# Block-sparse attention followed by a gated MLP on one core: probability transposes moved from TensorE to DMA, with converting loads, three score banks and a reordered start

## The chip, the cores and the metric

One core of a Trainium2 chip runs the whole program. The metric is the device time of one execution in microseconds (us). Below, PE is TensorE's matmuls and PEld its weight loads, DVE is VectorE, ACT is ScalarE, POOL is GpSimd, SP is SyncE; "SPq" or "POOLq" is the queue of instructions that such an engine issues, DMA issues above all.

## What is computed

Attention with a block mask (blocks of 32 rows, 24 blocks): a block sees itself and its neighbours, the first and the last block, and three sampled blocks; the first and the last block see everything. An MLP with a swish gate follows.

```python
batch, n_heads, seq, head_dim = (4, 8, 768, 64)
n_tokens, d_model, d_ff = (3072, 512, 2048)

scores = scale * np.matmul(q, k.transpose(0, 1, 3, 2))
mask = np.abs(blk_i - blk_j) <= window                     # window = 1
mask = mask | (blk_i == 0) | (blk_j == 0) | (blk_i == n_blocks - 1) | (blk_j == n_blocks - 1)
for qb in range(n_blocks):
    for kb in sampled_blocks[qb]:                          # three per block
        mask[qb * block:(qb + 1) * block, kb * block:(kb + 1) * block] = True
scores = np.where(mask, scores, -1000000000.0)
attn = softmax(scores)
x = (attn @ v) as (tokens, heads * head_dim)
h = x @ w_in
g = h * (1.0 / (1.0 + np.exp(-beta * h)))
out = g @ w_out
```

All inputs and the output are float32; the kernel works in float16 with float32 accumulation.

## The kernel before

**Tiles.** A batch's 768 queries are six chunks `c` of 128 (four blocks, index `j`). The eight heads go in two quads `Q` of four. A step is (batch, chunk, quad): 48 steps, twelve per batch, in the order of the list `steps`. The chunks come as 1, 2, 0, 5, 3, 4 (`CHUNK_ORDER`); chunks 0 and 5 hold the first and the last block, which need full rows.

**One step.** `scores` (matmuls on line 329) writes two score tiles `sc`, each one PSUM bank: for every block 96 window columns straight from `kT`, and 160 columns from `KG`, a gathered copy of K with the first block, three sampled blocks and the last block. DVE takes the negated maxima `nm` (line 334), ACT the exponentials `probs` (line 337), 128 x 1024 in float16. `probs_T` turns them with eight PE transposes (line 345) into the PSUM tile `tp_p`, which DVE copies to `probsT` (line 349). `attend` multiplies `probsT` by gathered V rows, `VA` (window and first block) and `VB` (sampled and last block), into `av` (line 397); V carries a column of ones, so the sums of the softmax come with it, and lines 415 and 416 divide. The full rows have their own path, `global_scores` (line 361, exponentials on line 375) and `global_T` (six transposes, line 384, and a DVE copy, line 387), four units per batch. `x_transpose` (lines 439 and 441) prepares the MLP's input when both quads of a chunk are done.

**MLP.** Chunks are grouped (`sizes`). For a group, `h_unit` does four matmuls (line 453), a tanh on ACT (line 457) and the gate on DVE (line 459); `o_unit` does half of a chunk's second product, eight matmuls (line 470), and with the second half ACT copies the result out (line 476). The units wait in `moe_q`, and `run_moe` spreads them over the steps, so that PE has matmuls while it waits for attention.

**Order.** The order on PE, POOL and SP is the order of the program text (`tc.manual_schedule`); DVE and ACT are placed by a scheduler. An engine takes its instructions in order, so that a waiting one holds up what stands behind it. `pend_T` and `pend_A` keep the transposition and the attend of a step behind its scores: a step's probabilities are transposed one step later, and attended about two steps later.

**Loads.** `load_quad` brings float32 K, Q or V into staging tiles. `prep_tensor` casts K and Q (ACT and DVE at the start, POOL later, line 212); `transpose_pair` makes `kT` and `qT` with six transposes of two heads at once (line 219) and an ACT copy (line 223). `prep_v` casts V, and `write_vtab` writes it to a table in HBM, `vtab` (line 239). `gather_v` reads rows of it: SP issues `VA` (lines 283, 286, 289) and `VB` (lines 294, 297, and one transfer per block and sample on line 300, their addresses held in registers), or, for chunk 1 alone, POOL issues four indirect transfers (line 280). `gather_chunk` builds `KG` on POOL (lines 255 and 261). The weights come as float32 into big staging tiles, w_in in two halves (line 179) and w_out in two (line 186), and DVE casts them (lines 181 and 188; w_out is halved there, which belongs to the tanh form of the gate).

**PSUM banks.** Scores two, transposes two (`tp_p`, `tp_g`, `tp_k`, `tp_q`, `tp_x` share them), `av` one, MLP three.

Of the kernel before, what the change touches and what calls it, by code (L numbers as in the profile page):

```python
# [20 lines left out]
def kernel(  # L21
# [30 lines left out]
    stage_pool = ctx.enter_context(tc.tile_pool(name="stage", bufs=3))  # L52
    half_pool = ctx.enter_context(tc.tile_pool(name="half", bufs=2))
# [14 lines left out]
    sc_psum = ctx.enter_context(tc.tile_pool(name="sc_psum", bufs=2, space=bass.MemoryType.PSUM))  # L68
    tp_psum = ctx.enter_context(tc.tile_pool(name="tp_psum", bufs=2, space=bass.MemoryType.PSUM))
# [86 lines left out]
    nc.vector.tensor_copy(out=idx_b, in_=idx_f)  # L156
# [18 lines left out]
    HF = D_FF // 2  # L175

    def load_w_in(hf, eng):
        wst = big("w_in_st").rearrange("p (c f) -> p c f", c=N_DMC)
        eng.dma_start(out=wst, in_=w_in_r[:, :, hf * HF:(hf + 1) * HF])
        for f0 in range(0, HF, 256):  # L180
            nc.vector.tensor_copy(out=w_in_sb[:, :, hf * HF + f0:hf * HF + f0 + 256],
                                  in_=wst[:, :, f0:f0 + 256])

    def load_w_out(hf):
        wst = big("w_out_st").rearrange("p (c m) -> p c m", m=D_MODEL)
        nc.gpsimd.dma_start(out=wst, in_=w_out_r[:, 8 * hf:8 * hf + 8, :])
        for c0 in range(0, 8, 2):
            nc.vector.tensor_scalar(out=w_out_sb[:, 8 * hf + c0:8 * hf + c0 + 2, :],
                                    in0=wst[:, c0:c0 + 2, :], scalar1=0.5, scalar2=None,
                                    op0=ALU.mult)  # L190
# [10 lines left out]
    def prep_tensor(name, b, Q, startup):  # L201
        st = st_tiles.pop((name, b, Q))
        h16 = half_pool.tile([P, 6, 4, D], FP16, tag="h16", name=f"{name}16")
        for h in range(4):
            dst = h16[:, :, h, :]
            src = st[:, h, :, :]
            if startup and name == "k":
                nc.scalar.copy(out=dst, in_=src)
            elif startup:
                nc.vector.tensor_copy(out=dst, in_=src)  # L210
            else:
                nc.gpsimd.tensor_copy(out=dst, in_=src)  # L212
        return h16

    def transpose_pair(name, b, Q, pr, h16):
        dstT = (qT if name == "q" else kT)[b]
        tp = tp_psum.tile([P, 1024], FP16, tag="tp", name=f"tp_{name}")
        for e in range(6):
            nc.tensor.transpose(out=tp[:, e * P:(e + 1) * P],  # L219
                                in_=h16[:, e, 2 * pr:2 * pr + 2, :].rearrange(  # L220
                                    "p h d -> p (h d)"),
                                identity=identity)
# [5 lines left out]
    def prep_v(b, Q, startup):  # L228
        st = st_tiles.pop(("v", b, Q))
        for h in range(4):  # L230
            eng = nc.vector if startup else nc.gpsimd
            last = eng.tensor_copy(out=v16[b][:, :, 4 * Q + h, 0:D], in_=st[:, h, :, :])
        return last
# [15 lines left out]
    def gather_chunk(b, c, KG, p0, p1):  # L249
# [3 lines left out]
        k_regs = load_regs(sb_raw, ET.Pool, NB - 1, c)  # L253
        for col, src in ((0, 0), (128, S - BLK)):
            nc.gpsimd.tensor_copy(  # L255
                out=KG[:, j0:j1, p0:p1, col:col + BLK],
                in_=kv[:, p0:p1, src:src + BLK].unsqueeze(1).to_broadcast(
                    [P, j1 - j0, p1 - p0, BLK]))
        for j in js:
            for r in range(3):  # L260
                last = nc.gpsimd.tensor_copy(  # L261
                    out=KG[:, j, p0:p1, BLK * (1 + r):BLK * (2 + r)],
                    in_=kv[:, p0:p1, bass.ds(k_regs[(4 * c + j, r)] * BLK, BLK)])
        return last

    def gather_v(b, c, indirect=False):
# [11 lines left out]
        if indirect:  # L278
            for j in js:
# [10 lines left out]
        if indirect:  # L290
            return VA, VB
        v_regs = load_regs(sb_eff, ET.SP, NB, c)
        gb = [j for j in js if 4 * c + j != NB - 2]
        nc.sync.dma_start(out=VB[96:128, gb[0]:gb[0] + len(gb), :],
                          in_=rows(S - BLK, BLK, 0, len(gb)))
        if len(gb) != nj:
            nc.sync.dma_start(out=VB[96:128, NB - 2 - 4 * c, :], in_=tab[S:S + BLK, :])
        for j in js:
            for r in range(3):
                nc.sync.dma_start(  # L300
                    out=VB[BLK * r:BLK * (r + 1), j, :],
                    in_=tab[bass.ds(v_regs[(4 * c + j, r)] * BLK, BLK), :])
# [38 lines left out]
    def probs_T(pt):  # L341
        tp = tp_psum.tile([P, 1024], FP16, tag="tp", name="tp_p")
        for u in range(4):
            for half in range(2):
                nc.tensor.transpose(out=tp[:, u * 256 + half * P:u * 256 + (half + 1) * P],  # L345
                                    in_=pt[:, u, half * P:(half + 1) * P],
                                    identity=identity)
        ptT = p_pool.tile([P, 4, 2, P], FP16, tag="probsT", name="probsT")
        nc.vector.tensor_copy(out=ptT.rearrange("p u h q -> p (u h q)"), in_=tp)  # L349
# [31 lines left out]
    def global_T(pg):  # L381
        tp = tp_psum.tile([P, 1024], FP16, tag="tp", name="tp_g")
        for ct in range(6):
            nc.tensor.transpose(out=tp[:, ct * P:(ct + 1) * P],
# [332 lines left out]
```

## Time and profile before

| | |
|---|---|
| median of 3 runs | 397.03 us (396.07 to 399.94) |
| profiled execution, own time | 399.42 us |
| its span | 397.6 us |
| mean granted PE clock | 0.966 |
| busy: PE, PEld, DVE, ACT, POOL | 310.0, 181.8, 239.3, 202.0, 170.6 us |
| moved by DMA | 61.24 MB, mean 154 GB/s |
| probs transposes on PE (line 345) | 384, 33.9 us |
| their copies on DVE (line 349) | 48, 32.2 us |
| global transposes on PE (line 384), copies on DVE (line 387) | 9.7 us, 8.8 us |
| K and Q transposes on PE (line 219), both | 192, 19.6 us |
| K and Q casts on POOL (line 212), both | 48, 23.4 us |
| weight casts on DVE (lines 181, 188) | 9.1 us, 5.7 us |
| indirect V gathers issued by POOL (line 280) | 16, 15.6 us |

The busy times come from the profile of one execution; matmuls overlap each other, so a busy PE is not PE at its peak. Where a stage is looked at alone, the busy time of each engine in that stretch of the span is asked for, and the waits and the chain are those that the profile infers from semaphores.

### The profile page before, as it was taken

To read this page: it belongs to the slowest core of one execution; us is meant where nothing else is said; L and a number is where in the kernel's file an instruction comes from. 1 tells how busy PE (TensorE), PEld (TensorE's weight loads), DVE (VectorE), ACT (ScalarE), POOL (GpSimd) and SP (SyncE) were. 2 spreads that over 40 slices of the span, in tenths; PEclk is the share of its full clock that TensorE was granted. 3 is DMA by queue.
4 is the path that set the end of the run, shared out by engine and by line. 5 is a ranking of instruction groups with operands and counts; after the bars stand their busy time and mean duration, and the time that the engine had idled before them with its cause. 6 is when DMAs were issued, how large, how long until landed. Compare 5 with 4: busy or idle time off the path is not lost.

```text
span 397.6 us, 12930 instructions
## 1 busy us (share of the span) xinstructions
PE 310.0 (78%) x5056; PEld 181.8 (46%) x5056; DVE 239.3 (60%) x499; ACT 202.0 (51%) x401; POOL 170.6 (43%) x472
## 2 busy tenths in 40 slices
PE   1433525685757778978988789999799999999996
PEld 0221313574544435444544455555454555445652
DVE  0938746864777664564777565667677767544330
ACT  3461313375645655542656666546555656444441
POOL 4748939957785194037780193082420400000000
PEclk9999999999978988996999999999899999999999
DMA  7798999756897233057983152454313424100112
GB/s 214 284 335 175 368 357 388 242 110 162 269 333 200 53 88 77 8 144 225 330 292 83 44 136 44 116 156 116 104 26 91 128 57 123 41 28 30 51 54 79
DMA packets 41085, 61.24 MB, mean 154 GB/s; under 512 B 7968, under 2 KB 31648, under 8 KB 41024
## 3 DMA queue, kind: packets, MB, share of 16 engines
q1 hardware_dynamic: 29136, 29.01, 27.9%
q0 software_dynamic: 6368, 25.11, 18.1%
q10 hardware_dynamic: 5520, 6.30, 4.6%
q8 instruction: 40, 0.66, 0.8%
q14 instruction: 21, 0.17, 0.1%
HBM read 50.77 MB, written 9.62 MB: 152 GB/s over the span
## 4 chain that ended last, share of the span: by engine, by line
PE 50%; DVE 23%; ACT 10%; DMA 8%; issue 3%; POOL 3%; another core or an unknown queue 1%; POOLq 0%; SPq 0%; ACTq 0%; DVEq 0%
PE ops L470 17%; PE hps L453 17%; DVE nm L334 6%; DMA w_out_st<-in_moe_w_out_dram 4%; DVE g L459 4%; PE sc L329 3%; PE tp_p L345 3%; ACT gp L375 3%; ACT t_sb L457 3%; ACT probs L337 3%; PE av L397 3%; DVE probsT L349 2%; DMA st_q<-in_q_dram 2%; PE av L409 2%; DVE gnm L369 2%
## 5 line engine op out<-in xcount | busy, mean ns | idle before, releaser
L337 ACT ACTIVATE probs<-sc,nm 128x256 f16<-128x256 f32 x192 | 75.5, 475 | 84.1 <-DVE nm L334 83.1
L459 DVE SCALAR_TENSOR_TENSOR g<-t_sb,hps 128x512 f16<-128x512 f16 (+1 forms) x112 | 67.9, 610 | 66.0 <-ACT t_sb L457 64.6
L453 PE MATMUL hps<-xT,w_in_sb 128*128 128x512 f16 (+1 forms) x448 | 101.3, 363 | 0.8 <-DVE g L459 0.7
L457 ACT ACTIVATE t_sb<-hps,beta_h_sb 128x512 f16<-128x512 f32 (+1 forms) x112 | 69.6, 630 | 49.1 <-PE hps L453 47.3
L470 PE MATMUL ops<-w_out_sb,g 128*128 128x512 f16 x384 | 91.9, 385 | 0.0
L334 DVE TENSOR_REDUCE nm<-sc 128x2 f32<-128x512 f32 x96 | 61.8, 684 | 28.1 <-PE sc L329 28.0
L261 POOL COPY KG<-kT 128x128 f16 (+1 forms) x288 | 72.5, 310 | 0.0
L453 PEld LDWEIGHTS <-w_in_sb 128*128 128x128 f16 x448 | 42.8, 102 | 36.0 <-issue 7.5
L470 PEld LDWEIGHTS <-g 128*128 128x128 f16 x384 | 37.5, 99 | 42.8 <-issue 3.4
L255 POOL COPY KG<-kT 128x512 f16<-128x512 f16 (+2 forms) x52 | 27.6, 562 | 48.8 <-PE sc L329 38.2
L329 PE MATMUL sc<-kT,qT 64*32 64x96 f16 (+1 forms) x832 | 24.4, 223 | 21.4 <-ACT gp L375 17.5
L329 PEld LDWEIGHTS <-qT 64*32 64x32 f16 x1536 | 17.0, 96 | 47.7 <-issue 29.3
L349 DVE COPY probsT<-tp_p 128x1024 f16<-128x1024 f16 x48 | 32.2, 671 | 7.5 <-remote 2.5
L280 POOL DMA_INDIRECT VB<-vtab,idx_b x16 | 15.6, 975 | 43.2 <-PE av L397 33.3
L345 PE MATMUL tp_p<-identity,probs 128*128 128x128 f16 x384 | 33.9, 239 | 0.0
L212 POOL CAST q<-st_q 128x384 f16<-128x384 f32 x24 | 11.2, 511 | 36.3 <-PE tp_k L219 18.5
L329 PE MATMUL sc<-KG,qT 64*32 64x160 f16 x704 | 22.2, 250 | 5.9 <-POOL KG L261 5.0
L476 ACT COPY osb<-ops 128x512 f32<-128x512 f32 x24 | 14.1, 588 | 24.3 <-PE ops L470 24.3
L345 PEld LDWEIGHTS <-probs 128*128 128x128 f16 x384 | 24.8, 107 | 3.2 <-issue 0.4
L375 ACT ACTIVATE gp<-scg,gnm 128x384 f16<-128x384 f32 x32 | 16.8, 577 | 17.9 <-DVE gnm L371 17.9
L397 PE MATMUL av<-VB,probsT 128*32 128x65 f16 x704 | 25.1, 203 | 0.1
L397 PE MATMUL av<-VA,probsT 128*32 128x65 f16 x704 | 23.2, 205 | 1.1 <-issue 1.1
(69 smaller groups left out, 306.6 us busy)
## 6 DMA issues: line engine op xcount, KB each, us to landing
VB<-vtab SPq DMA_DIRECT2D x220, 32.5 KB
VA<-vtab SPq DMA_DIRECT2D x16, 390.0 KB
out_dram<-osb ACTq DMA_DIRECT2D x24, 256.0 KB
st_v<-in_v_dram POOLq DMA_DIRECT2D x6, 768.0 KB
st_k<-in_k_dram POOLq DMA_DIRECT2D x6, 768.0 KB
st_q<-in_q_dram POOLq DMA_DIRECT2D x6, 768.0 KB
w_out_st<-in_moe_w_out_dram POOLq DMA_DIRECT2D x2, 2048.0 KB
VA<-vtab SPq DMA_DIRECT2D x8, 292.5 KB
```

The lines of the kernel that those rows point to most:

```text
L261: last = nc.gpsimd.tensor_copy(out=KG[:, j, p0:p1, BLK * (1 + r):BLK * (2 + r)], in_=kv[:, p0:p1, bass.ds(k_regs[(4 * c + j, r)] * BLK, BLK)])
L329: nc.tensor.matmul(o, lhsT=lhsT, rhs=rhs, start=True, stop=True, tile_position=(64 * hp, BLK * j))
L334: nc.vector.tensor_reduce(out=nm[:, hp, :], in_=scs[hp], axis=AX.X, op=ALU.max, negate=True)
L337: nc.scalar.activation(out=pt[:, 2 * pr + hp, :], in_=scs[hp][:, pr, :], func=AF.Exp, bias=nm[:, hp, pr:pr + 1], scale=1.0)
L345: nc.tensor.transpose(out=tp[:, u * 256 + half * P:u * 256 + (half + 1) * P], in_=pt[:, u, half * P:(half + 1) * P], identity=identity)
L349: nc.vector.tensor_copy(out=ptT.rearrange("p u h q -> p (u h q)"), in_=tp)
L375: nc.scalar.activation(out=pv[:, :, 64 * s:64 * (s + 1)], in_=halves[s].rearrange("p (s e) -> p e s", e=6), func=AF.Exp, bias=nm[:, 2:3], ...
L397: nc.tensor.matmul(av[BLK * j:BLK * (j + 1), u, :], lhsT=ptT[:, u, half, BLK * j:BLK * (j + 1)], rhs=V[:, j, h * VW:(h + 1) * VW], start=( ...
L453: nc.tensor.matmul(hp[:, 0:n], lhsT=w_in_sb[:, cc, f * P:(f + 1) * P], rhs=xT_tiles[gi][:, cc, 0:n], start=(cc == 0), stop=(cc == N_DMC - 1))
L457: nc.scalar.activation(out=t_sb[:, 0:n], in_=hp[:, 0:n], func=AF.Tanh, bias=0.0, scale=beta_h_sb[:, f:f + 1])
L459: nc.vector.scalar_tensor_tensor(out=g_tiles[gi][:, f, 0:n], in0=t_sb[:, 0:n], scalar=1.0, in1=hp[:, 0:n], op0=ALU.add, op1=ALU.mult)
L470: nc.tensor.matmul(op, lhsT=g_tiles[gi][:, f, s * P:(s + 1) * P], rhs=w_out_sb[:, f, :], start=(f == 0), stop=(f == N_FFC - 1))
```

## The change

- `probs_T` and `global_T` no longer use PE and DVE. SP issues one transposing DMA from `probs` to `probsT`, and from `gp` to `gpT`. It is issued in the step of the scores, and `pend_T` and `pend_G` are gone; `attend` runs two steps after the scores.
- Score banks three (two), transpose banks one (two).
- `load_w_in` and `load_w_out` become four transfers each, issued by POOL, from float32 in HBM straight into the float16 tiles; the halving of w_out moves to the copy of the result (`nc.scalar.mul(osb, op, 0.5)`).
- K and Q of later batches are loaded by converting POOL transfers into `h16` (four buffers); at the start one cast per tensor remains (`cast_quad`). `transpose_pair` makes twelve transposes of one head each, which write the upper or the lower 64 partitions.
- `gather_v` takes a list `direct` of the blocks whose rows SP issues; the others are POOL's indirect transfers. As a rule it is two and two; chunks 0 and 5 are all SP's in the first batch and all POOL's in the later ones. SP issues three transfers for each block of its share (line 300 of before).
- The start: the index arithmetic goes first on DVE (`tc.issue_after`), two V casts go to ACT, one half of a `KG` tile is gathered by DVE, and the first four attends and two global units run together in step 3. The weights follow the V gathers of the second chunk on POOL. The preparation of a later batch starts one step later.
- `sizes` is [2, 2, 4, 4, 4, 4, 2, 2] (was [2, 4, 4, 4, 4, 4, 2]).

```diff
-    stage_pool = ctx.enter_context(tc.tile_pool(name="stage", bufs=3))
-    half_pool = ctx.enter_context(tc.tile_pool(name="half", bufs=2))
+    stage_pool = ctx.enter_context(tc.tile_pool(name="stage", bufs=2))
+    half_pool = ctx.enter_context(tc.tile_pool(name="half", bufs=4))
...
-    sc_psum = ctx.enter_context(tc.tile_pool(name="sc_psum", bufs=2, space=bass.MemoryType.PSUM))
-    tp_psum = ctx.enter_context(tc.tile_pool(name="tp_psum", bufs=2, space=bass.MemoryType.PSUM))
+    sc_psum = ctx.enter_context(tc.tile_pool(name="sc_psum", bufs=3, space=bass.MemoryType.PSUM))
+    tp_psum = ctx.enter_context(tc.tile_pool(name="tp_psum", bufs=1, space=bass.MemoryType.PSUM))
...
+    def load_w_in(i):
+        nc.gpsimd.dma_start(out=w_in_sb[:, :, 512 * i:512 * (i + 1)],
+                            in_=w_in_r[:, :, 512 * i:512 * (i + 1)])
+
+    def load_w_out(i):
+        nc.gpsimd.dma_start(out=w_out_sb[:, 4 * i:4 * i + 4, :],
+                            in_=w_out_r[:, 4 * i:4 * i + 4, :])
...
+    def load_half(name, src, b, Q):
+        h16 = half_pool.tile([P, 4, 6, D], FP16, tag="h16", name=f"{name}16")
+        halves[(name, b, Q)] = h16
+        nc.gpsimd.dma_start(
+            out=h16.rearrange("p h e d -> p h (e d)"),
+            in_=src[b, 4 * Q:4 * Q + 4].rearrange("h (p e) d -> p h (e d)", p=P))
...
         for e in range(6):
-            nc.tensor.transpose(out=tp[:, e * P:(e + 1) * P],
-                                in_=h16[:, e, 2 * pr:2 * pr + 2, :].rearrange(
-                                    "p h d -> p (h d)"),
-                                identity=identity)
+            for hh in range(2):
+                nc.tensor.transpose(
+                    out=tp[64 * hh:64 * hh + 64, e * P:(e + 1) * P],
+                    in_=h16[:, 2 * pr + hh, e, :], identity=identity,
+                    tile_position=(0, 64 * hh))
...
-    def gather_v(b, c, indirect=False):
+    def gather_v(b, c, direct=()):
...
-        if indirect:
-            for j in js:
+        for j in js:
+            if j not in direct:
                 nc.gpsimd.indirect_dma_start(
                     VB[:, j, :], None, tab[:, :],
                     bass.IndirectOffsetOnAxis(idx_b[:, 4 * c + j:4 * c + j + 1], 0))
...
     def probs_T(pt):
-        tp = tp_psum.tile([P, 1024], FP16, tag="tp", name="tp_p")
-        for u in range(4):
-            for half in range(2):
-                nc.tensor.transpose(out=tp[:, u * 256 + half * P:u * 256 + (half + 1) * P],
-                                    in_=pt[:, u, half * P:(half + 1) * P],
-                                    identity=identity)
         ptT = p_pool.tile([P, 4, 2, P], FP16, tag="probsT", name="probsT")
-        nc.vector.tensor_copy(out=ptT.rearrange("p u h q -> p (u h q)"), in_=tp)
+        nc.sync.dma_start_transpose(ptT.rearrange("p u h q -> p (u h) q"),
+                                    pt.rearrange("p u k -> p (u k)"))
         return ptT
...
-        tp = tp_psum.tile([P, 1024], FP16, tag="tp", name="tp_g")
-        for ct in range(6):
-            nc.tensor.transpose(out=tp[:, ct * P:(ct + 1) * P],
-                                in_=pg[:, ct * P:(ct + 1) * P], identity=identity)
         gT = gpt_pool.tile([P, 6, P], FP16, tag="gpT", name="gpT")
-        nc.vector.tensor_copy(out=gT.rearrange("p c q -> p (c q)"), in_=tp[:, 0:S])
+        nc.sync.dma_start_transpose(gT, pg)
         return gT
...
+    alloc_batch(0)
+    with tc.issue_after(idx_done.ins):
+        for n in ("k", "q"):
+            cast_quad(n, 0, 0)
+            for pr in range(2):
+                transpose_pair(n, 0, 0, pr)
+        kg_half(0, 0)
+        kg_half(1, 0)
+        prep_v(0, 0, True)
+        prep_v(0, 1, True)
+    write_vtab(0, nc.sync)
+    prefetch_v(0, (0, 1))
+
+    def start_rest():
+        for n in ("k", "q"):
+            cast_quad(n, 0, 1)
+            for pr in range(2):
+                transpose_pair(n, 0, 1, pr)
+        prefetch_v(1, (0, 1))
+        load_w_in(0)
+        kg_half(0, 1, nc.vector)
+        kg_half(1, 1)
+        load_w_in(1)
+        load_w_in(2)
+        load_w_in(3)
...
         pt = scores(b, c, Q, KGs[(b, c)])
-        pend_T.append((b, c, Q, pt))
-        if len(pend_A) > 1:
+        pend_A.append((b, c, Q, probs_T(pt)))
+        if n == 3:
+            do_A()
             do_A()
-        if len(pend_T) > 1:
-            do_T()
+            do_G(0, 0)
+            do_A()
+            do_G(0, 1)
+            do_A()
+            do_X()
+            run_moe(len(moe_q) // 8)
+        elif n > 3 and len(pend_A) > 2:
+            do_A()
         run_moe(units // 4)
-        do_GT()
         if n == 0:
-            start_kq1()
-            start_kg(1)
-            load_w_in(1, nc.gpsimd)
-        if n == 2:
-            load_w_out(0)
-        if n == 4:
-            load_w_out(1)
+            start_rest()
+        if n in (3, 4):
+            load_w_out(2 * n - 6)
+            load_w_out(2 * n - 5)
...
         if Q == 1:
             ci = chunk_seq.index((b, c))
             prefetch(ci + 2)
-            prefetch_v(ci + 2)
+            direct = {0: (1, 2, 3), 5: (0, 1, 2)} if b == 0 else {0: (), 5: ()}
+            prefetch_v(ci + 2, direct.get(chunk_seq[(ci + 2) % 24][1], (0, 1)))
```

## Prediction

> **What bounds the kernel now.** I read the page's busy shares first, then the busy time by stage, then the chain of work that ended last, then SP's queue.
>
> ```profile
> PE 310.0 (78%) x5056; PEld 181.8 (46%) x5056; DVE 239.3 (60%) x499; ACT 202.0 (51%) x401; POOL 170.6 (43%) x472
> ...
> PE   1433525685757778978988789999799999999996
> ```
> ```profile
> 0.00:80.00 80.00, 33.58 (x613) 23.21 (x614) 49.11 (x110) 28.53 (x58) 56.16 (x154) 1.00 0.88 294
> 80.00:398.00 318.00, 276.44 (x4446) 158.55 (x4444) 190.19 (x389) 173.47 (x344) 114.43 (x318) 0.96 0.42 119
> ```
> The columns of the second fence are the stretch, its length, then PE, PEld, DVE, ACT, POOL busy, the granted clock, the DMA share and GB/s. There are two stages. Up to 80 us PE works 33.6 us and DMA is 88% busy: the first MoE matmul (line 453) starts at 79.98. After it PE is busy 276.4 of 317.6 us, 87%, and from 320 to 360 us it is 39.6 of 40: there PE is the bound.
>
> The chain in time order says what held the first stage:
>
> ```profile
> 37.75 17.23 DMA w_out_st<-in_moe_w_out_dram
> 55.00 2.50 DVE w_out_sb L188 x4
> 57.50 1.20 DVE nm L334 x2
> ```
> DVE runs in order, and the weight cast stands ahead of the score maxima, so a 2 MB load stops attention until 55 us.
>
> What the change takes from PE, and where it lies (busy time by stage again, PE and then DVE, of the instructions on tile tp_p, and then on tile tp_g):
>
> ```profile
> 80.00:398.00 318.00, 26.67 (x328) 27.43 (x41) 0.96 0.42 119
> ```
> ```profile
> 80.00:398.00 318.00, 6.33 (x72) 6.58 (x12) 0.96 0.42 119
> ```
> SP, which is to take the transposes, has this queue (start, length, what), and these waits in it:
>
> ```profile
> 229.30 4.40 SPq L300 DMA_DIRECT2D VB<-vtab  x9
> ```
> ```profile
> SPq L283 <- PE av L397: 77.2, 11, 10.7
> ```
> So an unhindered gather row costs SP 4.40/9 = 0.49 us; in the crowded opening 12 took 13.11, or 1.09 each.
>
> **The transpose itself, p.** The trace has no such operation. One probs tile is 128x1024 f16, 262 KB. Below: as bytes at the rate of the software queue,
>
> ```profile
> q1 hardware_dynamic: 29136, 29.01, 27.9%
> q0 software_dynamic: 6368, 25.11, 18.1%
> ```
> 25.11 MB in 18.1% x 16 x 397.6 = 1151 us of one engine, 349 KB/us over sixteen: 0.75 us. Above: if each 128-element row is a packet, 1024 packets at q1's mean, 27.9% x 16 x 397.6 / 29136 = 61 ns, over sixteen engines: 3.9 us, plus an issue like line 283's 0.34: 4.3. Between: q1's packets hold 996 bytes, and by bytes a quarter of 61 ns gives 1.0 us. I take p = 2.0, keeping 0.75 and 4.3; a 768-wide global tile is 0.75p.
>
> A rule speaks against the change. A probs transposition is eight 128x128 blocks, and the row is 0.62 us for a warm group of eight on PE. The Trainium skill, "VectorE: DVE Perf Modes", section "The three transpose paths", gives 1309 ns for one 128x128 block by DMA, and its rules table keeps to TensorE where PSUM can hold the result. If that grew with the blocks, p would be an estimated 10.5 us and 48 of them 503 us, far slower; if most of it is fixed, p stays near 2. "DMA: Bandwidth & Descriptors", section "Latency and other measured facts", has 261 GB/s for such transfers, which makes p an estimated 1.0 and the opening below 4 us earlier. No run here shows either yet.
>
> **Opening.** Removed: the w_in and w_out casts on DVE (9.1 + 5.7 us) with the load they wait for; the converting transfer writes the weight tiles directly. DVE now does all its index arithmetic first, about 5 us from 4.9, then q in one cast, then six V casts at 0.38 us while ACT does two. I put the write of vtab at 15, not 19.54; its landing takes 4.41, so V can be gathered from 19.5. Then SP's order decides: gathers of chunk 1, transposition, gathers of chunk 2, two transpositions, gathers of chunk 0, the fourth transposition. That is 21 rows at i each, eight other V issues of 0.3 to 0.5 us (3.8 in all), 4p, and 4 us from the last attend to MoE (before: av at 76.0, hps at 79.98). 19.5 + 3.8 + 4 + 21i + 4p: with i = 0.8 and p = 2, 52 us; with 0.49 and 0.75, 41; with 1.09 and 4.3, 67. First MoE at 52 is 28 earlier, but before had done eight scores by then and after has done four: four scores, two globals, one or two attends and 12 K transposes come later, some 5 us of PE. **-23** (-34 to -8). POOL issues w_in behind its first gathers and indirect rows; 4 MB at the 294 GB/s of this stage is 14 us, so it lands before 52.
>
> **After it.** 33.0 us of PE transposes go. What PE keeps of this depends on whether its queue is full: full share 33.0; none, 0 (second rival). I take the 87% that PE is busy: **-29**. The evictions (27.4 + 6.6 us of DVE here) go as well; DVE was not the bound, so nothing.
>
> K and Q are transposed per head: 134 transposes after 80 us become 268 on half the columns. If halves run side by side, 0; if not, tp_k and tp_q double, +11.8. The av matmuls, which also use part of the columns, overlap (32 in 0.45 us, though one takes 0.2), so **+3**. One transpose bank instead of two: a second pair in one step waits for ACT's eviction (0.81 us), three such steps in each of three batches, 0 to +7: **+2**.
>
> Three score banks: PE waited 17.5 us for the global exponentials to free a bank (9.4 of it after 100 us) and 16.4 for probs (3.3); 0 to -12.7: **-6**.
>
> POOL loses 23.4 us of casts and a half KG gather, and gains 34 indirect issues at 0.975 us, 33 us: about 177 of 350. Its idle half covers that; with the cover gone KG comes late, and PE already waits 5.0 us for it. Each indirect waits for a free VB, and behind it stand prep loads and the next KG, due two steps later. 0 to +10: **+1**. K and Q loads that convert, the 0.5 moved into line 476's copy (same 0.59 us) and the V casts stay hidden at nothing: the loads are issued two steps or more (13 us) ahead of their transposes. Without that cover each pair of loads would cost what lands late, a few us per batch.
>
> New wait: attend stands behind a DMA. It runs two steps after its scores; 40 steps took 82 to 346 us, 6.6 each, so some 12 us cover p plus queueing. SP waits for av before VA (77.2 us above), and now the next transposition is behind that wait, but the av it waits for is issued in the same step, ahead of those next scores. Uncovered cases in the global steps, two transposes each: 0 to +20, **+3**.
>
> Sum against the profiled span: 397.6 - 23 - 29 + 3 + 2 - 6 + 1 + 3 = 348.6. The execution lay 1.8 us over its span (399.42), and 2.4 over the median of the runs: **348.0**.
>
> **Rivals.** *SP becomes the bound (slower).* Per batch from the second on SP has four chunks of six direct rows (4.1 to 6.0 us each) and two of about 1.2, some 22 us, plus 15p. PE's pace after the change, 5.9 us a step, is 71 us a batch, so SP is full from p = 3.3. At 4.3 it is 86.5, 15.5 over, times 3.7 batches, +57: about 405; it is slower than before from p = 4.1. For it: if a quarter-size packet still costs 61 ns, 48 x 1024 + 16 x 768 = 61,440 packets put 234 us on the sixteen engines, beside 0.42 x 318 = 134 us there now after 80: more than the stage is long. Against: packets of a quarter of the bytes should not cost the same. Chance 0.13.
>
> *Only the opening gains.* The freed PE time turns into other waits: ACT already waits 83.1 us for the maxima, 46.9 of it after 100, and the chain's share of PE is only 50%. Then -29 is lost and the rest stands: 377. Against: 39.6 of 40 busy near the end, where nothing else can take over. Chance 0.20.
>
> *Everything at its good end:* opening -34, all 33.0, banks -12.7, the small costs at half: 322. Chance 0.09. It needs p below 1 and i near 0.49 while the w_in transfer shares the engines; the crowded 1.09 speaks against.
>
> **How the numbers follow.** The forecast has 0.58. About 1% is what a measurement of this kernel can tell from no change. Faster by over 1%: the forecast, the good end and most of the second rival, 0.84; slower 0.13; within 1% what is left of the second rival, 0.03. The range 326 to 390 leaves out the slow rival and part of the good end.
>
> **What would show it.** Right: first hps near 52; no tp_p or tp_g on PE, PE busy near 270 (310 - 43.6 + 3); PE over 87% after the first hps; a probs transposition landing within 5 us of its issue; w_out gone from the chain. The mid term is wrong if PE waits for probsT by DMA at line 397, the opening term if hps starts after 60. The forecast falls if SP has no idle time in the later batches.

## The result and the profile after

The changed kernel is slower: 435.29 us, median of 4 runs (430.33 to 436.38), against 397.80 us for the kernel before in the same comparison (396.07 to 399.94). The ratio is 1.0915, 95% interval 1.0814 to 1.1017. The forecast was 348.0 us, range 326 to 390. Some executions of a kernel run over one per cent longer than its others, and every ratio here is taken between the means of the others, so that it can differ a little from the ratio of the medians. The profiled execution took 436.38 us, with a span of 434.6 us.

The page after: busy time of PE, then the slices of PE, of its granted clock and of DMA.

```profile
PE 289.1 (67%) x4832; PEld 156.9 (36%) x4832; DVE 193.5 (45%) x441; ACT 203.9 (47%) x413; POOL 176.8 (41%) x449
...
PE   0440111755777075678815696888898999999996
...
PEclk9999999998888758799966898899989999999999
DMA  7899999958859999574999999347777994622101
```

PE does 20.9 us less work and DVE 45.8 less, as the change meant, but the span grew by 37. A slice is 10.9 us. The PE row has holes in the opening (up to some 76 us) and near 147 and 223 us; at the two later ones the clock row dips as well, to 5 and 6 tenths.

Busy time by stage, cut at the first MoE matmul (stretch, length, PE, PEld, DVE, ACT, POOL, granted clock, DMA share, GB/s):

```profile
0.00:75.90 75.90, 16.00 (x377) 10.57 (x378) 22.25 (x73) 19.59 (x33) 45.60 (x125) 1.00 1.07 224
75.90:434.60 358.70, 273.11 (x4456) 146.29 (x4455) 171.23 (x368) 184.34 (x380) 131.18 (x325) 0.90 0.76 142
```

Before, the cut was at 80 us and 317.6 followed it. So the opening gained 4 us and the rest lost 41. In the rest PE is busy 76% of the time (87% before): 85.6 us idle against 41.2. The DMA share went from 0.42 to 0.76 for 23 GB/s more. The queues say which transfers these are:

```profile
q1 hardware_dynamic: 86032, 38.11, 48.7%
q0 software_dynamic: 14672, 22.82, 27.4%
```

The queue of SP has 56,896 more packets than before (29,136). 61,440 are the transpositions: 1024 packets of 256 bytes for each of 48 probs tiles and 768 for each of 16 global ones.

The longest waits of PE, of the whole span and then after 80 us (who waited for whom, us in all, times, longest), and last the longest one of the kernel before:

```profile
PE av L387 <- DMA probsT<-probs: 72.4, 12, 15.4
PE sc L328 <- ACT gp L369: 9.3, 8, 3.0
```
```profile
PE av L387 <- DMA probsT<-probs: 35.4, 8, 10.6
```
```profile
PE sc L329 <- ACT gp L375: 17.5, 24, 2.0
```

The wait for probsT did not exist before. 37.0 us of it are in the opening, and 29.3 of the other 35.4 at the two changes of batch under which loads run (135 to 160 and 230 to 247 us). For the opening, SP's queue in order of time (start, length, what):

```profile
23.80 3.91 SPq L299 DMA_DIRECT2D VB<-vtab  x5
27.81 1.44 SPq L342 DMA_TRANSPOSE probsT<-probs  x1
...
32.76 4.63 SPq L299 DMA_DIRECT2D VB<-vtab  x6
38.01 7.39 SPq L342 DMA_TRANSPOSE probsT<-probs  x2
...
50.77 11.35 SPq L299 DMA_DIRECT2D VB<-vtab  x9
62.33 1.27 SPq L342 DMA_TRANSPOSE probsT<-probs  x1
63.70 7.70 SPq L377 DMA_TRANSPOSE gpT<-gp  x2
```

For the changes of batch, PE in order of time; in brackets the idle time just before and what ended it:

```profile
136.02 3.25 PE L460 MATMUL ops<-w_out_sb,g 128*128 128x512 f16 x8
...
140.46 0.43 PE L328 MATMUL sc<-KG,qT 64*32 64x160 f16 x8
151.45 0.25 PE L387 MATMUL av<-VA,probsT 128*32 128x65 f16 x4 [10.56 <-DMA probsT<-probs]
...
158.83 3.60 PE L460 MATMUL ops<-w_out_sb,g 128*128 128x512 f16 x8
```

PE takes its instructions in order, so for 10.56 us no MoE matmul runs either. Eight matmuls of line 460 then take 3.60 us; eight of them take 1.89 at 387.31, when the clock is full. The eight at 136.02, ahead of this stall, took 3.25, so the clock was low there already.

Nine transpositions, worked out from the trace's records of SP's instructions and of the 256-byte packets (us from the span's start):

```
step  probs ready  issued  first packet  last packet  PE idle before av
  1       30.1      38.0       41.9          48.7          14.5
  3       36.1      62.3       66.3          69.8          15.4
 12      133.2     141.9      143.7         149.4          10.6
 13      137.9     143.3      149.3         155.5           1.0
 22      214.6     217.5      218.8         227.9          10.6
 23      218.7     218.9      228.1         237.4           3.0
 24      223.2     240.8      242.7         244.9           3.8
 42      351.8     351.8      353.1         354.5           0.0
 47      391.9     391.9      393.1         394.5           0.0
```

"Issued" is the start of SP's issue. Undisturbed (42, 47) a transposition has its first packet 1.2 to 1.3 us after that, and 1.4 us of data. Step 3 waited 26.2 us for its issue, behind the transpositions of steps 1 and 2 and the V transfers of the next chunk, the nine rows of line 299 among them; steps 12, 13, 22 and 23, when the next batch's loads are under way, had 5.7 to 9.3 us of data. All 48: from probabilities to the last packet 6.3 us in the median, 8.2 in the mean, 33.7 at worst (step 3). The signal that PE waits for comes 0.5 us after the last packet when nothing disturbs (step 47) and 3.2 us after it in step 3.

### The profile page after: what moved, and what is told of

Read it like the earlier page. It is cut to its first block, busy times and chain, and to the rows that moved or that the text cites. A ratio compares the mean times of both kernels' runs of the same rounds, so it can differ in the third digit from the quotient of the medians.

```text
span 434.6 us, 12281 instructions
## 1 busy us (share of the span) xinstructions
PE 289.1 (67%) x4832; PEld 156.9 (36%) x4832; DVE 193.5 (45%) x441; ACT 203.9 (47%) x413; POOL 176.8 (41%) x449
## 4 chain that ended last, share of the span: by engine, by line
PE 40%; DMA 25%; ACT 13%; DVE 9%; SPq 9%; issue 2%; another core or an unknown queue 1%; ACTq 0%
PE hps L443 16%; PE ops L460 15%; DMA VA<-vtab 11%; DMA probsT<-probs 8%; ACT probs L336 6%; DVE g L449 3%; DMA VB<-vtab 3%; ACT t_sb L447 3%; SPq L342 3%; DVE nm L333 3%; PE av L387 2%; PE sc L328 2%; SPq L377 2%; SPq L299 2%; DMA beta_sb<-in_moe_beta_dram 2%
## 5 line engine op out<-in xcount | busy, mean ns | idle before, releaser
L447 ACT ACTIVATE t_sb<-hps,beta_h_sb 128x256 f16<-128x256 f32 (+1 forms) x128 | 72.4, 585 | 101.2 <-PE hps L443 97.2
L443 PE MATMUL hps<-xT,w_in_sb 128*128 128x256 f16 (+1 forms) x512 | 112.9, 363 | 5.7 <-DVE g L449 5.1
L449 DVE SCALAR_TENSOR_TENSOR g<-t_sb,hps 128x256 f16<-128x256 f16 (+1 forms) x128 | 69.5, 552 | 94.4 <-ACT t_sb L447 92.3
L280 POOL DMA_INDIRECT VB<-vtab,idx_b x50 | 48.4, 968 | 123.5 <-PE av L387 113.2
L460 PE MATMUL ops<-w_out_sb,g 128*128 128x512 f16 x384 | 95.6, 396 | 0.0
L387 PE MATMUL av<-VA,probsT 128*32 128x65 f16 x704 | 23.1, 208 | 75.2 <-DMA probsT<-probs 72.4
L387 PEld LDWEIGHTS <-probsT 128*32 128x32 f16 x1408 | 18.3, 102 | 83.4 <-DMA probsT<-probs 76.0
L405 DVE RECIPROCAL rec<-av 128x4 f32<-128x4 f32 x48 | 8.5, 176 | 67.5 <-PE av L387 61.8
L466 ACT ACTIVATE osb<-ops 128x512 f32<-128x512 f32 x24 | 14.3, 598 | 23.7 <-PE ops L460 22.0
L363 DVE TENSOR_REDUCE gnm<-scg 128x1 f32<-128x384 f32 x32 | 17.1, 552 | 18.0 <-PE scg L355 15.4
L216 PE MATMUL tp_k<-identity,k 128*64 128x128 f16 x192 | 11.3, 273 | 18.0 <-ACT k L199 9.2
L216 PE MATMUL tp_q<-identity,q 128*64 128x128 f16 x192 | 10.0, 249 | 18.7 <-ACT qT L220 8.8
```

Source lines behind the costliest of these rows:

```text
L216: nc.tensor.transpose(out=tp[64 * hh:64 * hh + 64, e * P:(e + 1) * P], in_=h16[:, 2 * pr + hh, e, :], identity=identity, tile_position=(0, ...
L280: nc.gpsimd.indirect_dma_start(VB[:, j, :], None, tab[:, :], bass.IndirectOffsetOnAxis(idx_b[:, 4 * c + j:4 * c + j + 1], 0))
L387: nc.tensor.matmul(av[BLK * j:BLK * (j + 1), u, :], lhsT=ptT[:, u, half, BLK * j:BLK * (j + 1)], rhs=V[:, j, h * VW:(h + 1) * VW], start=( ...
L443: nc.tensor.matmul(hp[:, 0:n], lhsT=w_in_sb[:, cc, f * P:(f + 1) * P], rhs=xT_tiles[gi][:, cc, 0:n], start=(cc == 0), stop=(cc == N_DMC - 1))
L447: nc.scalar.activation(out=t_sb[:, 0:n], in_=hp[:, 0:n], func=AF.Tanh, bias=0.0, scale=beta_h_sb[:, f:f + 1])
L449: nc.vector.scalar_tensor_tensor(out=g_tiles[gi][:, f, 0:n], in0=t_sb[:, 0:n], scalar=1.0, in1=hp[:, 0:n], op0=ALU.add, op1=ALU.mult)
```

## The experiments

Four theories. A: the transpositions' packets fill the DMA engines, land late, and PE waits in order and then runs at a lower clock. B: another part (converting loads, V sharing, the new start) is the loss. C: SP's queue is the place: a transposition stands behind gather rows and their waits. D: the engines serve a bulk load and a transposition in turn, so that one beside a load takes many times its data. The kernel before ran at 388.7 to 389.7 us (medians) on the chips of the experiments, so ratios are compared.

**e1_pe_T: all of the change but the transposes.**

```diff
-        nc.sync.dma_start_transpose(ptT.rearrange("p u h q -> p (u h) q"),
-                                    pt.rearrange("p u k -> p (u k)"))
+        tp = tp_psum.tile([P, 1024], FP16, tag="tp", name="tp_p")
...
+                nc.tensor.transpose(out=tp[:, u * 256 + half * P:u * 256 + (half + 1) * P],
+                                    in_=pt[:, u, half * P:(half + 1) * P],
+                                    identity=identity)
...
+        nc.vector.tensor_copy(out=ptT.rearrange("p u h q -> p (u h q)"), in_=tp)
```

The global tiles likewise; the transposes run one step after the scores, with two score banks and two transpose banks.

> The changed kernel with its transposes of probs and gp put back on PE and DVE, one step after the scores, and the banks back at two and two; converting loads, V sharing and the reordered start stay. Theory A (the 61,440 transposing packets fill the DMA engines, so probsT lands late, PE waits in order and its clock falls): most of the loss goes, 375 to 395 us, DMA share after 80 us near 0.5, granted clock back at 0.96 or more, no wait of PE on probsT by DMA. Theory B (the converting loads, the V sharing or the new start are what fills DMA): stays at 415 to 435. Theory C (SP's in-order queue alone): near 390 too, so this run does not tell A from C.

Measured: 377.65 us (375.47 to 378.22), ratio 0.9694 [0.9619, 0.9769]. Its busy time by stage, cut at its first MoE matmul:

```profile
0.00:47.90 47.90, 19.94 (x421) 14.38 (x422) 25.19 (x79) 19.28 (x33) 33.81 (x98) 1.00 0.96 240
47.90:376.40 328.50, 288.60 (x4892) 173.02 (x4891) 205.47 (x426) 184.56 (x380) 142.34 (x351) 0.95 0.48 124
```

The rest of the change is a gain of 3%: B falls. PE is busy 19.4 us longer than in the changed kernel (308.5 in all) but idle 67.9 us instead of 145.5: 77.6 less, close to the 72.4 of waiting for probsT. SP's nine rows now take this, 0.60 us each instead of 1.26:

```profile
37.99 5.41 SPq L299 DMA_DIRECT2D VB<-vtab  x9
```

**e2_dma_T: only the transposes, in the kernel before.**

```diff
-        pend_T.append((b, c, Q, pt))
-        if len(pend_A) > 1:
+        pend_A.append((b, c, Q, probs_T(pt)))
+        if len(pend_A) > 2:
             do_A()
-        if len(pend_T) > 1:
-            do_T()
```

`probs_T` and `global_T` are those of the changed kernel.

> The kernel before with only the transposes of probs and gp moved to a transposing DMA from SP, issued in the step of the scores, attends two steps after the scores; banks, loads, V gathers and start as before. Theory A: slower than before, 415 to 440 us, with PE waiting for probsT by DMA over 40 us in all. Theory B: 370 to 390, since PE loses 43.6 us of transposes and the converting loads are absent. Theory C: slower still than the changed kernel, 440 or more, because SP here also issues all of the sampled V rows, 220 instead of 114.

Measured: 471.83 us (464.55 to 475.41), ratio 1.2014 [1.1881, 1.2147].

```profile
PE av L388 <- DMA probsT<-probs: 130.2, 22, 24.9
```

Here SP also issues all the sampled rows but chunk 1's. From probabilities to issue takes 7.8 us in the median, against 1.0 in the changed kernel, while the data takes 1.4. That speaks for the queue (C) as a cost of its own, which the V sharing of the change would then have repaired in part; but e2 lacks the rest of the change too.

**e3b_conv_all: only the converting loads, in the kernel before.**

```diff
-    def load_w_out(hf):
...
+    def load_w_out(hf):
+        for i in (2 * hf, 2 * hf + 1):
+            nc.gpsimd.dma_start(out=w_out_sb[:, 4 * i:4 * i + 4, :],
+                                in_=w_out_r[:, 4 * i:4 * i + 4, :])
```

The same for w_in, K and Q; K and Q are transposed per head.

> The kernel before with only the converting loads: w_in, w_out and the K and Q of later batches come by POOL straight into float16, the 0.5 of w_out moves to the output copy, K and Q are transposed per head; transposes of probs on PE, V gathers and order of the start as before. Theory A: faster than before, 378 to 392 us, as DVE no longer waits for a weight load ahead of the score maxima (the chain held 17.2 us of it) and converting costs DMA little. Theory B: slower than before, 405 to 425.

Measured: 379.62 us (378.80 to 387.07), ratio 0.9763 [0.9672, 0.9854]. The first MoE matmul moves from 79.98 to 68.9, and 308.1 us follow it (317.6 before). The packets of all queues take 210.1 us per engine (204.9 before): converting costs the DMA engines next to nothing. B falls here too.

**e6_all_pool: the changed kernel, sampled V rows from the third chunk on by POOL.**

```diff
-            direct = {0: (1, 2, 3), 5: (0, 1, 2)} if b == 0 else {0: (), 5: ()}
-            prefetch_v(ci + 2, direct.get(chunk_seq[(ci + 2) % 24][1], (0, 1)))
+            prefetch_v(ci + 2)
```

> The changed kernel with all sampled V rows of the third chunk on gathered by POOL's indirect transfers, so that SP issues only the VA rows and the transposes there; same bytes, 102 DMA issues fewer on SP. Theory A: the DMA engines stay full and PE keeps waiting for probsT, 425 to 440 us. Theory C (a transposition waits in SP's queue behind gather rows): PE's waits for probsT fall by half or more, 395 to 415.

Measured: 417.10 us (412.43 to 421.72), ratio 1.0685 [1.0553, 1.0817]. Neither expectation came: more is gained than A allowed, but PE's wait for probsT stays (72.1 us). From probabilities to issue takes 1.7 us in the mean instead of 3.2, and yet to the last packet 8.2 as before: what was won in SP's queue was lost behind it.

**e5_spread: the changed kernel, next batch's loads over five steps instead of two.**

```diff
-        items[o] += [lambda: alloc_batch(b), load_v(0), load_v(1), load("k", 0),
-                     load("k", 1)]
+        items[o] += [lambda: alloc_batch(b), load_v(0)]
+        items[o + 1] += [load_v(1), load("k", 0)]
```

The second K quad follows in o + 2, the first Q quad and the table in o + 3, the second Q quad in o + 4.

> The changed kernel with the next batch's loads issued over five steps instead of three, at most two of them in a step. Theory A with D (each packet of a load delays one packet of a transposition, and only what exceeds the two steps of slack is lost): the bursts of 10 to 16 us at the batch changes shrink under the slack, the ratio to before falls from 1.09 to 1.04 to 1.07. Rival (SP's queue order is what counts, not the loads): unchanged, 1.08 to 1.10.

Measured: 412.21 us (411.71 to 414.42), ratio 1.0637 [1.0581, 1.0693].

**e13_spread_pool: both of these edits together.**

> The changed kernel with both cures at once: next batch's loads spread over five steps, and all sampled V rows from the third chunk on by POOL, so that SP issues only VA and transpositions there. If collision with loads and SP's order are two separate costs: the gains add, 1.092 - 0.028 - 0.023 = 1.041, about 405 us (399 to 410). If both cures remove the same waits: 1.06, 410 to 416. If these two are the whole cost of the transposition by DMA: the level of the PE version or below, 0.97, at most 380.

Measured: 407.99 us, but the four runs lay from 392.89 to 417.38, with clocks from 0.943 to 0.875, and no ratio can be given. The stages of the profiled executions tell more (first MoE matmul; what follows it in the span; PE's wait for probsT):

```
                     first hps   rest of span   PE waits for probsT
before                 80.0         317.6             -
after                  75.9         358.7           72.4
e6_all_pool            59.4         354.4           72.1
e5_spread              70.4         339.5           62.8
e13_spread_pool        61.2         338.1           53.3
e1_pe_T                47.9         328.5             -
```

The rows on SP cost 16.5 us in the opening and 4.3 later, which is less than the changed kernel's runs differ among themselves; the loads cost 19.2 later and 5.5 in the opening. With both edits each stage is near the better of the two. That speaks for separate costs (C and D), but as one execution of a kernel whose runs differ by 6% it does not show it. 13.3 us of the opening and some 10 of the rest remain. The wait of 72.1 us in e6 hardly differs from the 72.4, though 21 us of span are gained: a sum of waits is not a price.

**m1_price: the transposition by itself.** A kernel that leaves out the whole computation (its output is zeros): eight transpositions of 128x1024 from SP, three times, the second meant to lie beside plain loads of w_in in float32 and the third beside converting ones.

```diff
+    for n in range(8):
+        nc.sync.dma_start_transpose(o, src[i])
...
+    for i in range(4):
+        nc.gpsimd.dma_start(out=wide[:, i, :], in_=w_r[:, i, :])
...
+    for i in range(4):
+        nc.gpsimd.dma_start(out=half[:, i, :], in_=w_r[:, i, :])
```

> A kernel of its own that leaves the whole computation out (its output is zeros): three bursts of eight 128x1024 transposing DMAs from SP, the first with nothing else moving, the second beside a plain 4 MB float32 load from POOL, the third beside the same load converted to float16. Theory D (an engine that has two queues takes their packets in turn, so each 256-byte packet of a transposition waits for one packet of the load): 1.4 us of data for each transposition in the quiet burst, 9 to 13 beside plain packets of 4 KB at some 170 ns, 6 to 8 beside converted ones of 1 KB at some 96 ns. Rival (the crossbar itself is slow or the bandwidth is shared by bytes): beside both loads the same, 2 to 4 us.

Measured (85.44 us); SP's queue, start, length, what:

```profile
1.96 14.93 SPq L42 DMA_TRANSPOSE quiet<-src  x8
30.94 18.75 SPq L42 DMA_TRANSPOSE plain<-src  x8
65.09 15.75 SPq L42 DMA_TRANSPOSE conv<-src  x8
```

Alone, one has 1.40 to 1.43 us of data (the first two). The rest did not fall as meant. Each load began while the burst ahead of it was ending, and the writes of the zeros ran through most of the kernel. So the transposition beside the plain load is the last of the first burst, and the one beside the converting load the last of the second.

Worked out from the trace's packets, the one beside the plain load has 12.0 us of data. In it start 366 load packets of 8192 bytes, 23 per engine at 328 ns, and 509 packets of the zeros at 88 ns; with its own 64 per engine at 26 ns they make 7.5 + 2.8 + 1.7 = 12.0 us of each engine. Beside the converting load it is 13.05 us, with 364 load packets of 4096 bytes at 389 ns and 377 of the zeros. So the time that D gave for a plain load came out, but by luck: the packets were twice as large as it took them to be, and about a third as many passed. Its figure for converting loads, 6 to 8 us beside packets of 1 KB, was not tried here, because no such packets occur. The changed kernel has them: while the weights load, the transpositions of steps 1 and 2 have 6.80 and 7.01 us of data, in which 1042 and 1064 load packets of 1024 bytes start, one for each of their own 1024. This is D's figure, and the counts fit its mechanism.

The Trainium skill, "DMA: Bandwidth & Descriptors", section "Queues, rings and completion order", has each engine taking packets from its queues in turn; the counts in steps 1 and 2 agree with it.

**e9_slack3: the changed kernel, attends three steps after the scores.**

```diff
-    p_pool = ctx.enter_context(tc.tile_pool(name="probs", bufs=3))
-    gp_pool = ctx.enter_context(tc.tile_pool(name="gprobs", bufs=2))
+    p_pool = ctx.enter_context(tc.tile_pool(name="probs", bufs=4))
+    gp_pool = ctx.enter_context(tc.tile_pool(name="gprobs", bufs=1))
...
-    o_pool = ctx.enter_context(tc.tile_pool(name="osb", bufs=2))
+    o_pool = ctx.enter_context(tc.tile_pool(name="osb", bufs=1))
...
-        elif n > 3 and len(pend_A) > 2:
+        elif n > 3 and len(pend_A) > 3:
```

> The changed kernel with attends three steps after their scores instead of two (one more buffer for probs and probsT, one less for the output copy and for gp). If the loss is latency that a deeper queue hides, PE's waits for probsT after 90 us fall by half or more and the ratio to before goes from 1.09 to 1.03 to 1.06. If the DMA engines or SP are simply full for long stretches, a step more of slack is used up as well: 1.07 to 1.10.

Measured: 442.27 us (439.32 to 444.12), ratio 1.1391 [1.1321, 1.1462]. Who waits here:

```profile
PE av L387 <- DMA probsT<-probs: 65.3, 12, 16.1
...
ACT gp L369 <- DMA gpT<-gp: 48.6, 6, 25.2
```

The memory for a fourth probs buffer came from the second gp buffer, and the exponentials then waited for a transposition. From probabilities to issue now takes 5.8 us in the median (1.0). So this run doesn't say what a later attend alone would bring.

**e11, e12, e10: the transpositions by DMA in one stage only.** All are e1 with DMA transposition in some of the steps n and PE transposes elsewhere: n < 4 in e11_open_dma, 4 <= n < 36 in e12_mid_dma and n >= 36 in e10_late_dma. The cut is of e11; e10 writes the condition out. In e10 POOL also fetches the last batch's sampled rows.

```diff
+    def by_dma(n):
+        return n < 4
...
+        if not by_dma(n):
+            pend_T.append((b, c, Q, pt))
+        else:
+            while pend_T:
+                do_T()
+            pend_A.append((b, c, Q, probs_T_dma(pt)))
```

> The kernel with PE transposes (377.7 us, first MoE matmul at 47.9) but with the six transpositions of the first four steps by DMA from SP, as in the changed kernel; everything later stays on PE. Theory: these transpositions stand in SP's queue behind gather rows and share the sixteen DMA engines with the weight and next-batch loads, so the opening pays here what it paid in the changed kernel: first MoE matmul at 68 to 76, the time after it as before (328 +- 4), total 398 to 406, ratio 1.02 to 1.045. Rival (one transpose bank, three score banks or the V share, not the DMA, delayed the start): first MoE matmul at 47 to 52, total 376 to 382, ratio 0.97 to 0.98.

> The same kernel with DMA transpositions only in steps 4 to 35 and the global units of those batches, PE transposes in the opening and in the last batch. Theory: the loss after the opening sits where loads of the next batch are under way, so the first MoE matmul stays near 48 and the stretch after it grows from 328.5 to 355 to 365, total 404 to 414, ratio 1.04 to 1.065. Rival (only the opening loses; later the two steps of slack cover the transposition): stretch 318 to 330, total 368 to 380, ratio 0.945 to 0.98.

> As the run with PE transposes, but in the last batch, where no loads of K, Q, V or weights are left, probs and gp are transposed by DMA in the step of their scores, and POOL gathers all sampled V rows of that batch, so that SP's queue is short. Theory A with D: with quiet DMA engines the transposition costs PE nothing, and the 12 x 0.62 + 4 x 0.5 = 9 us of PE work is saved in a stage where PE is full: 366 to 372 us by the scale on which the PE-transposing run is 377.7 and before 388.7, and no waits for probsT there. Rival (DMA transposes hold PE up wherever they are): 378 to 390.

Measured: e11 399.45 us (395.64 to 403.11), ratio 1.0207 [1.0119, 1.0296]; e12 406.32 us (404.07 to 413.66), 1.0449 [1.0372, 1.0525]; e10 372.88 us (368.46 to 373.89), 0.9565 [0.9506, 0.9623]. Where the first MoE matmul stands (its line's count, durations, first and last start) and how long PE waits for probsT, in e11 and then in e12:

```profile
L463 PE MATMUL hps<-xT,w_in_sb x512: 269/379/634, 74.2 to 382.5; 128*128 128x256 f16 x86, 128*128 128x512 f16 x85
```
```profile
PE av L407 <- DMA probsT<-probs: 37.1, 4, 15.1
```
```profile
L463 PE MATMUL hps<-xT,w_in_sb x512: 269/379/634, 47.6 to 389.0; 128*128 128x256 f16 x86, 128*128 128x512 f16 x85
```
```profile
PE av L407 <- DMA probsT<-probs: 49.4, 13, 14.5
```

Six transpositions in the opening move the first MoE matmul from 47.9 to 74.2, where the changed kernel has it (75.9), with two transpose banks as well. Those of steps 4 to 35 leave the opening alone and lengthen what follows from 328.5 to 354.7. In e10 PE has no wait for probsT among its waits, and the edit pays: from 270 us to the end PE is busy 92.5 us against 97.4 in e1, in 102.0 us against 106.4. That POOL fetches more rows belongs to this edit and was not tried alone. By ratios against e1: +0.051, +0.076 and -0.013 make 0.969 + 0.114 = 1.083; the changed kernel has 1.0915, from 1.0814 on. The three stages account for the loss within the intervals. All three have two score and two transpose banks, so little is left for the banks as a cause.

**e14_from30: DMA transposition from step 30 on**, behind the steps that issue the last loads (25 to 27).

```diff
+        return n >= 30
...
+            prefetch_v(ci + 2, () if ci + 2 >= 15 else
+                       direct.get(chunk_seq[(ci + 2) % 24][1], (0, 1)))
```

> The mixed kernel (372.9 us) with DMA transpositions from step 30 on instead of 36, the first step after the last loads have landed; sampled V rows by POOL from the chunk of step 30 on. Theory (transposition by DMA pays where no load is under way): six more steps at the saving of the twelve, 4.8/12 = 0.4 us each, so 370.5 (368 to 373), ratio 0.945 to 0.955. Rival (what paid was the tail after the last loads and gathers alone, or POOL's added rows cost as much): 373 to 378, ratio 0.957 to 0.97.

Measured: 368.95 us (367.42 to 370.70), ratio 0.9503 [0.9455, 0.9552]. This is the fastest version, ahead of both kernels. It lies below e10 by 0.006, though the intervals overlap. Here too POOL took over rows.

## Why the prediction was wrong, by its own steps

The span was missed by 86 us (434.6 against 348.6): 19 in the opening and 67 after it.

**The new wait (+3, bounds 0 to +20): the step that failed.** It set 12 us of cover against p plus queueing, all means. The mean would have fitted: 8.2 us. But the queueing comes in bursts, just where it costs most: 16.1 us from probabilities to the last packet in step 12, 17.6 in step 13, 18.7 in step 23. PE waited 35.4 us after 80 us, above the upper bound, and e12 prices the steps 4 to 35 at 26 us after the first MoE matmul although PE's transposes are saved there. The wait that the prediction argued about, VA's for av, did become small (15.9 us in all, 77.2 before). It left out that SP is held by the transpositions themselves. Step 24 took 17.6 us to its issue, and this stood ahead of it in SP's queue, right behind the transpositions of steps 22 and 23:

```profile
221.14 0.58 SPq L283 DMA_DIRECT2D VA<-vtab  x1
221.77 8.43 SPq L286 DMA_DIRECT2D VA<-vtab  x1
...
231.68 8.99 SPq L299 DMA_DIRECT2D VB<-vtab  x6
```
```profile
SPq L299 <- DMA probsT<-probs: 7.8, 3, 4.1
```
One VA transfer took 8.43 us to issue, while in e1 no gather takes more than 1.42, and of the 8.99 us of the six rows 4.1 were a wait until a probsT had landed.

**p = 2.0 (bounds 0.75 to 4.3).** As data it held: median 2.0, mean 2.7, undisturbed 1.4. The error was to take the length of the data for the delay. Ahead of it stands 1.2 us from the start of the issue to the first packet, during which SP is busy with the issue (1.25 us), and beside a load the data takes four to nine times as long. Against the 1309 ns for one block in the Trainium skill, "VectorE: DVE Perf Modes", section "The three transpose paths", eight blocks need 2.6 us from the start of the issue when nothing disturbs, so most of that figure is fixed and not per block. The same page's rule, in section "Rules for kernel authors", to use TensorE if the result may go to PSUM held here for the kernel as a whole, by e1 against the changed kernel, but not behind the last loads, by e10 and e14.

**Opening (-23, bounds -34 to -8).** The new order is worth more than I forecast, by itself: 80.0 to 47.9 in e1, where I had put 52. With the transpositions the first MoE matmul stands at 75.9, a gain of 4. Two terms of the formula failed. 4p was 8 us; from issue to last packet the four took 6.0, 10.7, 15.8 and 7.4, two of them overlapping. And i = 0.8: 20 of the 21 rows took 3.91 + 4.63 + 11.35 us, 1.0 each, and the last nine, ahead of the fourth transposition, 1.26. The rows took 0.5 to 0.6 in e1. The transpositions are part of the reason: 3.4 of the 11.35 us were a wait until that of step 2 had landed. They are not all of it, as the first six rows, ahead of any transposition, took 0.74 each already. The formula also left out the two global transpositions of step 3, 7.70 us of SP; they stand behind the fourth one and held up the next chunk's rows.

**PE transposes (-29 of 33.0).** The work went, but PE kept little. After the first MoE matmul its busy time fell by only 3.3 us (276.4 to 273.1) and its idle time grew by 44. Some 7 us of the missing gain are work that moved over from the opening, where PE's busy time fell by 17.6 us, 10.6 of them transposes. A larger reason: the MoE matmuls took 112.9 + 95.6 = 208.5 us, 15.3 more than before, at a mean clock of 0.90 instead of 0.96. That they are 896 now and were 832 is not the reason, since e1 has 896 too and needs 193.1. The forecast of "PE busy near 270" missed by 19, mostly for this reason. "PE over 87%" gave 76.

**The small terms.** K and Q per head (+3): tp_k and tp_q together went from 19.7 to 21.4 us, 1.7 more, so it was near enough. One transpose bank (+2, 0 to +7): PE's waits for ACT to evict K and Q sum to 19.6 us after 80, where before its waits for a bank summed to 10.3; undersized, if none of it overlaps, and not tried alone. Three score banks (-6): the wait for the global exponentials went from 17.5 to 9.3 and that for probs left the longest seven; what it is worth in time wasn't tried alone. POOL (+1): covered, and e6 put 34 more indirect rows on it (209.5 us busy) and gained. Converting loads at nothing: they are a gain, by e3b.

**Rivals.** *SP becomes the bound* has the nearest time, 405, and the right sign, but not the mechanism: SP isn't full. Its longest waits, but for the kernel's end, are for work that ACT has not done yet, 40.5 us of them at line 342 (the profile names ACT's last instruction ahead of the release). It is late only in bursts.

```profile
SPq L342 <- ACT t_sb L447: 40.5, 14, 8.0
```
*Only the opening gains* (377) was right that PE's freed time turns into other waits, but here the opening gained only 4 us, and the rest lost 41.

**The signs to look for.** Two were well chosen and both came: PE waiting for probsT, and hps after 60. "Landing within 5 us of its issue" held for 34 of the 48, by their last packet.

## What to carry to other kernels

Price a DMA that replaces an engine's work by its delay at the busiest moment, not by its bytes or by a mean: list the bulk loads under way when it is issued, everything ahead of it in its issuing queue, and what it holds up behind it there. When the consumer stands in an in-order queue that also feeds the bound engine, a late landing stops all the work behind it. Use such transfers where the DMA engines are quiet; here the same instruction cost 8% between steps 4 and 35, and brought 1 to 2% in the last third, there together with rows that moved to POOL.

## What the runs showed of the hardware

- A 128x1024 float16 transposition from SBUF to SBUF: 1.25 us of issue on SP, the first packet 1.2 us after the start of the issue, 1.4 us of data alone. Beside converting loads in packets of 1024 bytes the data took 6.80 and 7.01 us, one load packet for each of its own; in m1_price, beside packets of 8192 and 4096 bytes and the writes of the zeros, 12.0 and 13.05 us. Issued back to back in the opening, a second one held SP for 5.46 us.
- The clock falls with PE's waits, and not only with the longest. From 150 to 160 us, during and behind the last of the stall of 10.56 us, the granted clock was 0.50; from 136.0 to 138.5 us, behind a wait of 2.41 us, it was 0.50 too. The Trainium skill, "TensorE: Matmul & The Clock Gate", section "Part 1: The HAM clock gate (the "warmup" mystery)", has the clock fall to half after an idle window of some 3.4 us; the long stall agrees with it. No run here separates what the clock adds from what the waits cost.
- In the opening the clock row can't be relied on. It reads 1.00 up to 97 us, but at 80.97 us eight matmuls of line 443 on 256 columns took 1.89 us, and at 386.44 us, 1.03.
